# Gate logits of four steps on four column tiles of 32, turned back in one product into another PSUM bank

## The chip, the cores and the metric

The kernel runs on one core of a Trainium2 chip. The core has five engines with a queue each: PE (TensorE, products), DVE (VectorE), ACT (ScalarE), POOL (GpSimd) and SP (SyncE, which here issues DMAs). An engine takes its instructions in order and waits on semaphores. The metric is the device time of one execution in microseconds. Three runs of the kernel before took 274.95, 274.98 and 278.34 us, median 274.98.

## The reference

Two parts, one behind the other, in f32. First a recurrence over 768 tokens, for 4 sequences and 8 heads of width 48:

```
for t in range(S):
    cur = u * k_t (outer) v_t
    y[:, :, t] = r_t @ (state + cur)
    state = w * state + k_t (outer) v_t
```

Its output, as 3072 tokens of width 384, goes through a layer with 8 experts, each token to one of them:

```
do_compute = x @ w_skip > 0
logits = x[do_compute] @ w_gate            # 8 of them
e_idx = argmax(logits); gate_w = softmax(logits)[e_idx]
out = x + gate_w * (relu(x @ w1[e_idx]) @ w2[e_idx])      # where do_compute, else x
```

The eight logits and the skip score of a token are the nine numbers that this change is about.

## The kernel before, in words

*Stages.* The first stage runs over 24 steps (`NT`), numbered n: 2 pairs of sequences, 12 steps of 64 tokens each. A step handles 64 tokens of two sequences, which is 128 rows of x. The second stage computes the experts with weights that are loaded and split into a high and a low part during the first stage and behind it. Between them `route` sorts tokens to experts, from the logits in `lg`, in four groups of steps: 0 to 8, 8 to 16, 16 to 20, 20 to 24 (`GROUPS`).

*The order of work.* It is written out by hand: the loop over n issues the functions below in the order of the code, and each engine's queue holds its instructions in just that order. PE's work in step n is: `scores(n+1)` (L441, 32 records on 64x64 tiles of the array, into ps_p), `across(n+1)` (L527, state times r, into ps_y), `turn_k(n+2)` (L454, four transposes into ps_l), in some steps `gate_back`, `turn_x(n)` (L569, three transposes of x into ps_t), `state(n+1)` (L474, into ps_s), in some steps `gate_some`, and `within(n+1)` (L503, into ps_y). DVE masks the scores behind each `scores` (L462, L463), which frees ps_p and gives `within` its weights, builds rd for later steps (L411, L419) and does the many small steps of `route`. ACT copies what PE leaves in PSUM: kt (L456), xT (L572), sblk (L483), x (`evac`, L538), and makes the high parts of the weights (L113). POOL builds kd three steps ahead (L429) and the low parts (L114). SP issues the loads of dm and v five and four steps ahead, the stores of x, and one piece of expert weights a step.

*The logits.* `turn_x(n)` leaves x transposed in xT, which holds four steps (`GB`). When four are there (n = 3, 7, 11, 15, 19), `gate_some(n)` multiplies them with the gate weights wgp, zero-padded to 64 columns. Since the 384 columns of x belong to two halves c of 64 tokens, the products of c = 0 go to partitions 0 to 63 of ps_l and those of c = 1 to 64 to 127, six products in all (three parts j of the contraction), each with 256 moving columns (four steps of 64 tokens). ACT copies the result to lt. In the next step `gate_back(n)` turns it back, so that tokens lie on partitions: two products of lt with `pick`, a table of ones and zeros that also takes the nine wanted columns, into the free columns 384 and up of ps_t, the bank of `turn_x`; ACT copies from there into `lg`. A sixth call at n = 22 handles three steps (20 to 22), and its `gate_back` is issued behind the loop; the last step has a `gate` of its own (L581).

*Names.* ps_p (two banks), ps_y (two banks), ps_s, ps_r, ps_t and ps_l are all of PSUM. ps_r is used by `route` alone in the first stage (L673 to L683, L794, L796, L750), and by the experts behind it. wk, tab are pools in SBUF. A product of f32 shows in the profile as two records, an L474 of 8 products as x16.

Of the kernel before, what the change touches and what calls it, by code (L numbers as in the profile page):

```python
# [59 lines left out]
def tile_wkv_moe(  # L60
# [183 lines left out]
    with ExitStack() as actx:  # L244
# [125 lines left out]
        def setup_routes():  # L370
            nc.vector.memset(before, 0.0)
            rows = ident.rearrange("p (c q e) -> p c q e", c=2, q=NB)[:, :, :, : E + 1]
# [189 lines left out]
        gts, xcopy = {}, {}  # L562
        seen = [-1]

        def turn_x(n):
            x = xts.pop(n)
            pt = ps_t if n + 1 < NT else ps_y[:, 0]
            for c in range(NCC):
                nc.tensor.transpose(pt[:, c * P : (c + 1) * P], x[:, c * P : (c + 1) * P], ident)  # L569
            if n % GB == 0:  # L570
                gts[0] = wk.tile([P, NCC, 2, GB, C], F32, tag="xT", name=f"xT{n}", bufs=1)
            xcopy[n] = nc.scalar.copy(  # L572
                gts[0][:, :, :, n % GB, :], pt[:, :DM].rearrange("p (j c t) -> p j c t", j=NCC, c=2)
            ).ins

        def gate(n):
            half = slice(n % 2 * C, (n % 2 + 1) * C)
            pg = ps_y[half, 0, DM : DM + NB * (E + 1)]
            for j in range(NCC):
                for c in range(2):  # L580
                    nc.tensor.matmul(  # L581
                        pg,
                        gts[0][:, j, c, n % GB, :],
                        wgp[:, j, c].rearrange("p (q e) -> p q e", q=NB)[:, :, : E + 1],
                        start=(j == c == 0),
                        stop=(j == NCC - 1 and c == 1),
                    )
# [5 lines left out]
        def gate_some(n, k=GB):  # L593
            pg = ps_l[:, : k * C]
            for j in range(NCC):
                for c in range(2):
                    nc.tensor.matmul(  # L597
                        pg[c * C : (c + 1) * C, :],
                        wgp[:, j, c, :],
                        gts[0][:, j, c, :k, :].rearrange("p k t -> p (k t)"),  # L600
                        start=(j == 0),
                        stop=(j == NCC - 1),
                        skip_group_check=True,
                    )
            lt = turned_lg[n] = wk.tile([P, GB * C], F32, tag="lt", name=f"lt{n}", bufs=1)[:, : k * C]
            nc.scalar.copy(lt, pg)

        def gate_back(n, k=GB):
            lt = turned_lg.pop(n)
            w = NB * (E + 1)  # L610
            for j in range(0, k, 2):
                m = min(2, k - j) * C
                nc.tensor.matmul(
                    ps_t[:m, DM + j // 2 * w : DM + (j // 2 + 1) * w],
                    lt[:, j * C : j * C + m],
                    pick.rearrange("p q e -> p (q e)"),
                    start=True,
                    stop=True,
                )
            g0, full = n - k + 1, k // 2 * 2  # L620
            nc.scalar.copy(
                lg[:, g0 : g0 + full, :].rearrange("p n e -> p (n e)"), ps_t[:, DM : DM + full // 2 * w]
            )
            if k > full:
                nc.scalar.copy(
                    lg[:C, g0 + full : g0 + full + 2, :].rearrange("p n e -> p (n e)"),
                    ps_t[:C, DM + full // 2 * w : DM + (full // 2 + 1) * w],
# [272 lines left out]
        load_v(4)  # L900
        prep_r(2)
# [3 lines left out]
        for n in range(NT - 1):  # L905
# [368 lines left out]
def _layout(r, k, v, w, u, moe_w_skip, moe_w_gate, moe_w1, moe_w2):  # L1274
# [19 lines left out]
    gq = np.zeros((2, NB * NHP * D, NB, C // NB), wide.dtype)  # L1294
    for q in range(NB):
        gq[:, q * NHP * D : (q + 1) * NHP * D, q, : E + 1] = wide
    gq = gq.reshape(2, NCC, P, C).transpose(2, 1, 0, 3)
# [38 lines left out]
```

## Time and profile before

| | |
|---|---|
| three runs, median | 274.98 us |
| profiled execution: time, and span of its profile | 276.32 us, 274.2 us |
| PE busy | 255.6 us (93%) |
| DVE, ACT, POOL busy | 183.2, 141.1, 131.4 us |
| first stage, to the end of `within(23)` and the turning of x behind it | about 124.6 us of the span |
| granted clock of TensorE, mean | 0.998 |
| DMA over the span | 54.30 MB, mean 198 GB/s |

The profile is of one execution. A row of the chain of waits gives a start in us, a length in us, and the line whose work the end of the program depended on at that time. A row of a timeline gives start and length of a run of equal instructions, the engine, the line, the operation, the tiles (out<-in) and their shapes; in brackets stands the idle time of the engine before it and what ended that. PEld is the loading of weights into the array. Ends of PE's records are modelled, their starts are not. "128*64" ahead of a shape is the tile of the array: 128 rows, 64 columns.

### The profile page before, as it was taken

To read this page: it belongs to the slowest core of one execution; us is meant where nothing else is said; L and a number is where in the kernel's file an instruction comes from. 1 tells how busy PE (TensorE), PEld (TensorE's weight loads), DVE (VectorE), ACT (ScalarE), POOL (GpSimd) and SP (SyncE) were. 2 spreads that over 40 slices of the span, in tenths; PEclk is the share of its full clock that TensorE was granted. 3 is DMA by queue.
4 is the path that set the end of the run, shared out by engine and by line. 5 is a ranking of instruction groups with operands and counts; after the bars stand their busy time and mean duration, and the time that the engine had idled before them with its cause. 6 is when DMAs were issued, how large, how long until landed. Compare 5 with 4: busy or idle time off the path is not lost.

```text
span 274.2 us, 8740 instructions
## 1 busy us (share of the span) xinstructions
PE 255.6 (93%) x3545; PEld 233.9 (85%) x3545; DVE 183.2 (67%) x372; ACT 141.1 (51%) x316; POOL 131.4 (48%) x131
## 2 busy tenths in 40 slices
PE   7998999999979989788999999999999999999990
PEld 2797897878869877776879999999999999999990
DVE  8786657598896899954655686757748377483310
ACT  2664566667756756434455554717548085480300
POOL 8536313375545538511748853763525535255011
PEclk9999999999999999999999999999999999999999
DMA  7977678878999995435479994694837747100010
GB/s 201 308 197 240 163 203 277 248 247 256 289 274 282 272 284 159 114 93 143 111 254 308 365 379 166 219 317 145 260 121 241 241 142 261 43 4 27 15 35 23
DMA packets 31140, 54.30 MB, mean 198 GB/s; under 512 B 4535, under 2 KB 14412, under 8 KB 31088
## 3 DMA queue, kind: packets, MB, share of 16 engines
q1 hardware_dynamic: 28896, 48.19, 57.2%
q0 software_dynamic: 2048, 5.44, 5.8%
q8 instruction: 30, 0.49, 0.7%
q14 instruction: 22, 0.18, 0.2%
q10 hardware_dynamic: 144, 0.00, 0.0%
HBM read 45.82 MB, written 8.65 MB: 199 GB/s over the span
## 4 chain that ended last, share of the span: by engine, by line
PE 82%; DVE 10%; ACT 3%; issue 2%; DMA 1%; POOL 0%; POOLq 0%; ACTq 0%
PE ps_p L164 11%; PE ps_y L164 11%; PE ps_p L441 8%; PE ps_p L154 5%; PE ps_r L154 5%; PE ps_l L154 5%; PE ps_y L154 5%; PE ps_s L474 5%; PE ps_y L503 5%; PE ps_l L454 4%; PE ps_y L527 3%; PE ps_l L597 3%; PE ps_t L569 3%; PE ps_y L216 2%; PE ps_p L216 2%
## 5 line engine op out<-in xcount | busy, mean ns | idle before, releaser
L114 POOL TENSOR_TENSOR lo<-raw,hi 128x512 fp32r<-128x512 f32 x42 | 57.0, 1358 | 75.3 <-ACT hi L113 55.7
L113 ACT CAST hi<-raw 128x512 fp32r<-128x512 f32 x96 | 55.1, 624 | 0.0
L114 DVE TENSOR_TENSOR lo<-raw,hi 128x512 fp32r<-128x512 f32 x54 | 44.0, 837 | 2.6 <-ACT hi L113 2.3
L429 POOL TENSOR_TENSOR kd<-dm,w_d 128x512 f32<-128x512 f32 x22 | 30.1, 1366 | 14.7 <-DMA dm<-in_dm_dram 13.0
L172 POOL DMA_INDIRECT out_dram<-xg,sid x16 | 17.1, 1067 | 36.4 <-DVE xg L169 25.7
L462 DVE COPY_PREDICATED am<-below,ps_p 128x512 f32<-128x512 int8 x24 | 17.7, 739 | 17.1 <-PE ps_p L441 17.0
L441 PE MATMUL ps_p<-rd,kd 64*64 64x128 f32 x768 | 26.9, 276 | 0.3 <-issue 0.3
L441 PEld LDWEIGHTS ps_p<-rd,kd 64*64 64x64 f32 x768 | 20.9, 132 | 3.2 <-issue 0.7
L158 ACT ACTIVATE hh<-ps_p 128x464 fp32r<-128x464 f32 x7 | 3.9, 559 | 36.9 <-PE ps_p L154 20.1
L122 POOL DMA_INDIRECT xg<-out_dram,gid x16 | 18.2, 1139 | 8.7 <-DVE gw L694 4.0
L503 PE MATMUL ps_y<-vz,am 128*64 128x96 f32 x384 | 20.2, 247 | 2.1 <-DVE am L463 1.5
L503 PEld LDWEIGHTS ps_y<-vz,am 128*64 128x64 f32 x384 | 17.8, 137 | 3.4 <-issue 1.9
L405 ACT ACTIVATE rd<-rd,uw 128x128 f32<-128x128 f32 x52 | 17.8, 395 | 4.9 <-DVE rd L411 4.9
L474 PE MATMUL ps_s<-vz,kt 128*64 128x96 f32 x352 | 19.6, 253 | 0.0
L456 ACT COPY kt<-ps_l 128x512 f32<-128x512 f32 x22 | 12.8, 583 | 12.9 <-PE ps_l L454 12.9
L164 PE MATMUL ps_p<-hi,hh 128*128 128x384 f32 x56 | 19.4, 347 | 0.0
L164 PE MATMUL ps_y<-hi,hh 128*104 128x384 f32 x56 | 18.9, 338 | 0.0
L164 PE MATMUL ps_p<-hi,hl 128*128 128x384 f32 x56 | 18.9, 337 | 0.0
L164 PE MATMUL ps_y<-lo,hh 128*104 128x384 f32 x56 | 18.9, 337 | 0.0
L164 PE MATMUL ps_y<-hi,hl 128*104 128x384 f32 x56 | 18.9, 337 | 0.0
L164 PE MATMUL ps_p<-lo,hh 128*128 128x384 f32 x56 | 18.8, 336 | 0.0
L169 DVE SCALAR_TENSOR_TENSOR xg<-ps_y,gate_s,xg 104x384 f32<-104x384 f32 (+1 forms) x8 | 4.9, 616 | 20.5 <-PE ps_y L164 17.9
(244 smaller groups left out, 693.4 us busy)
## 6 DMA issues: line engine op xcount, KB each, us to landing
raw<-in_w_dram SPq DMA_DIRECT2D x96, 256.0 KB
dm<-in_dm_dram SPq DMA_DIRECT2D x24, 512.0 KB
vz<-in_tok_dram SPq DMA_DIRECT2D x48, 96.0 KB
out_dram<-xt SPq DMA_DIRECT2D x48, 96.0 KB
out_dram<-xt SPq DMA_DIRECT2D x4, 192.0 KB
xg<-out_dram,gid POOLq DMA_INDIRECT x16
out_dram<-xg,sid POOLq DMA_INDIRECT x16
wgp<-in_wgq_dram SPq DMA_DIRECT2D x1, 192.0 KB
```

The source lines that it names most:

```text
L113: nc.scalar.copy(hi, t)
L114: eng.tensor_tensor(lo, t, hi.bitcast(F32), ALU.subtract)
L122: ins = nc.gpsimd.indirect_dma_start(out=xg, out_offset=None, in_=out[0:rows], in_offset=bass.IndirectOffsetOnAxis(ap=gid[:, q : q + 1], a ...
L154: nc.tensor.matmul(ph, a[:, c, fs], b[:, c, :], start=(k == 0), stop=(k == 3 * NCC - 1))
L164: nc.tensor.matmul(py, a, b[:, f, :], start=(k == 0), stop=(k == 3 * NFC - 1))
L172: ins = nc.gpsimd.indirect_dma_start(out=out, out_offset=bass.IndirectOffsetOnAxis(ap=sid[:, q : q + 1], axis=0), in_=xs.pop(q), in_offset ...
L405: nc.scalar.mul(rd[:, :, 1], rd[:, :, 0], uw[:, hp : hp + 1])
L429: (eng or nc.gpsimd).tensor_tensor(kds[n], d[:, 1], w_d[:, n % NSUB, 1][:, :, None].to_broadcast([DR, NHP, 2, C]), ALU.mult,)
L441: nc.tensor.matmul(ps_p[q * C : (q + 1) * C, a, 2 * hp * C : 2 * (hp + 1) * C], kd[h, hp, q, :], rd[h, hp, q].rearrange("p s c -> p (s c)" ...
L462: nc.vector.copy_predicated(shape(am[n % 2]), below, p[:, :, 0])
L474: nc.tensor.matmul(s[a * C : (a + 1) * C, :, hp * D : (hp + 1) * D], kt[:, hp, a, :], t[:, :, a, hp, :], start=i == 0 and hp == 0, stop=Tr ...
L503: ins = nc.tensor.matmul(place_y(a, c)[:, :, g, :], am[n % 2][:, a, hp * C : (hp + 1) * C], t[:, :, a, hp, :], start=g == 0 and n % NSTEP ...
```

## The change

Five edits.

1. wgp has 32 columns for a pair of steps and half (18 are used: two sets of nine) in place of 64, so its load is 96 KB, not 192 KB. The load is issued behind `load_v(4)`, in the program's opening, where it was behind `load_v(3)`.
2. `gate_some` makes twelve products in place of six: for each j and c one for steps 0 and 1 and one for steps 2 and 3 of the four (i), each with 128 moving columns, into partitions 32(2c + i) and up of ps_l. Its result is 128 columns wide, not 256, and the copy to lt too. At n = 22 all four steps of xT are multiplied, the fourth being an old one.
3. `pick` is twice as wide, and `gate_back` makes one product of 36 columns, into the last columns of ps_r, not ps_t.
4. In the loop, `gate_some` at n = 3, 7, 11, 15 and 19 comes behind `within(n+1)` and `evac(n+1)`; at n = 22 it stays ahead of `within`.
5. xT is one fixed tile in place of one taken anew from a pool every four steps.

```diff
-        wgp = tab.tile([P, NCC, 2, C], F32, name="wgp")
-        nc.sync.dma_start(out=wgp, in_=wgq)
-        pick = tab.tile([P, NB, E + 1], F32, name="pick")
+        wgp = tab.tile([P, NCC, 2, C // 2], F32, name="wgp")
+        pick = tab.tile([P, 2, NB, E + 1], F32, name="pick")
...
         def gate_some(n, k=GB):
-            pg = ps_l[:, : k * C]
+            pg = ps_l[:, : 2 * C]
+            w = C // 2
             for j in range(NCC):
                 for c in range(2):
-                    nc.tensor.matmul(
-                        pg[c * C : (c + 1) * C, :],
-                        wgp[:, j, c, :],
-                        gts[0][:, j, c, :k, :].rearrange("p k t -> p (k t)"),
-                        start=(j == 0),
-                        stop=(j == NCC - 1),
-                        skip_group_check=True,
-                    )
-            lt = turned_lg[n] = wk.tile([P, GB * C], F32, tag="lt", name=f"lt{n}", bufs=1)[:, : k * C]
+                    for i in range(2):
+                        nc.tensor.matmul(
+                            pg[(2 * c + i) * w : (2 * c + i + 1) * w, :],
+                            wgp[:, j, c, :],
+                            xT4[:, j, c, 2 * i : 2 * i + 2, :].rearrange("p k t -> p (k t)"),
+                            start=(j == 0),
+                            stop=(j == NCC - 1),
+                            skip_group_check=True,
+                        )
+            lt = turned_lg[n] = wk.tile([P, 2 * C], F32, tag="lt", name=f"lt{n}", bufs=1)
             nc.scalar.copy(lt, pg)
 
         def gate_back(n, k=GB):
             lt = turned_lg.pop(n)
             w = NB * (E + 1)
-            for j in range(0, k, 2):
-                m = min(2, k - j) * C
-                nc.tensor.matmul(
-                    ps_t[:m, DM + j // 2 * w : DM + (j // 2 + 1) * w],
-                    lt[:, j * C : j * C + m],
-                    pick.rearrange("p q e -> p (q e)"),
-                    start=True,
-                    stop=True,
-                )
+            pb = ps_r[:, 512 - 2 * w :]
+            nc.tensor.matmul(pb, lt, pick.rearrange("p s q e -> p (s q e)"), start=True, stop=True)
...
         load_v(4)
+        nc.sync.dma_start(out=wgp, in_=wgq)
         prep_r(2)
...
-            if n < TE and n % GB == GB - 1:
-                gate_some(n)
-            elif n == NT - 2:
+            if n == NT - 2:
                 gate_some(n, NT - 1 - TE)
             within(n + 1, kcopy.get(n + 2, xcopy[n]))
             evac(n + 1)
+            if n < TE and n % GB == GB - 1:
+                gate_some(n)
             if back:
                 back()
```

How this stands on PE, from `turn_x(3)` in step 3 to `state(5)` in step 4, in the kernel before; kd, rd, kt, xt and the like carry numbers of their buffers:

```order
L569 MATMUL ps_t<-ident,xt_523 128x128 x3
L474 MATMUL ps_s<-vz_128,kt_495 64x2x48 x8
L597 MATMUL ps_l<-xT_333,wgp 64x256 x6
L503 MATMUL ps_y<-vz_128,am_151 64x2x48 x8
L441 MATMUL ps_p<-rd_503,kd_501 64x128 x16
L527 MATMUL ps_y<-sblk_200,rd_503 64x48 x16
L454 MATMUL ps_l<-ident,kd_582 128x128 x4
L613 MATMUL ps_t<-pick,lt_602 128x18 x2
L569 MATMUL ps_t<-ident,xt_612 128x128 x3
L474 MATMUL ps_s<-vz_129,kt_576 64x2x48 x8
```

The same stretch of PE in the changed kernel, whose lines are numbered a little lower (L453 is `turn_k`, L473 `state`, L502 `within`, L440 `scores`, L526 `across`):

```order
L569 MATMUL ps_t<-ident,xt_523 128x128 x3
L473 MATMUL ps_s<-vz_128,kt_495 64x2x48 x8
L502 MATMUL ps_y<-vz_128,am_150 64x2x48 x8
L597 MATMUL ps_l<-xT_200,wgp 32x128 x12
L440 MATMUL ps_p<-rd_503,kd_501 64x128 x16
L526 MATMUL ps_y<-sblk_199,rd_503 64x48 x16
L453 MATMUL ps_l<-ident,kd_582 128x128 x4
L612 MATMUL ps_r<-pick,lt_620 128x36
L569 MATMUL ps_t<-ident,xt_604 128x128 x3
L473 MATMUL ps_s<-vz_129,kt_576 64x2x48 x8
```

L597 has moved from between L474 and L503 to between L503 and L441, with twelve products of half the columns on half the width; `gate_back`'s product has become one, into ps_r.

On ACT, from the copy of xT in step 3 to the copy of lg in step 4, before:

```order
L572 COPY xT_333<-ps_t 128x6x64
L483 COPY sblk_200<-ps_s 128x384
L606 COPY lt_602<-ps_l 128x256
L538 COPY xt_612<-ps_y 128x384
L405 ACTIVATE rd_584<-rd_584,uw 128x2x64 x2
L456 COPY kt_662<-ps_l 128x512
L621 COPY lg<-ps_t 128x36
```

And in the changed kernel:

```order
L570 COPY xT_200<-ps_t 128x6x64
L482 COPY sblk_199<-ps_s 128x384
L537 COPY xt_604<-ps_y 128x384
L606 COPY lt_620<-ps_l 128x128
L404 ACTIVATE rd_584<-rd_584,uw 128x2x64 x2
L455 COPY kt_668<-ps_l 128x512
L614 COPY lg<-ps_r 128x36
```

The copy of lt now stands behind the copy of x, ahead of the bonus (L404), and lg is read from ps_r; kt's copy is still ahead of lg's.

More of the change, by code (lines that the diff above doesn't have):

```diff
@@ L371, in setup_routes @@
             nc.vector.memset(before, 0.0)
-            rows = ident.rearrange("p (c q e) -> p c q e", c=2, q=NB)[:, :, :, : E + 1]
+            rows = ident.rearrange("p (c s q e) -> p c s q e", c=2, s=2, q=NB)[:, :, :, :, : E + 1]
             nc.vector.tensor_tensor(pick, rows[:, 0], rows[:, 1], ALU.add)
@@ L560, in put_x @@
                 x_out.append(ins.ins)
-        gts, xcopy = {}, {}
+        xT4 = tab.tile([P, NCC, 2, GB, C], F32, name="xT4")
+        xcopy = {}
         seen = [-1]
@@ L569, in turn_x @@
                 nc.tensor.transpose(pt[:, c * P : (c + 1) * P], x[:, c * P : (c + 1) * P], ident)
-            if n % GB == 0:
-                gts[0] = wk.tile([P, NCC, 2, GB, C], F32, tag="xT", name=f"xT{n}", bufs=1)
             xcopy[n] = nc.scalar.copy(
-                gts[0][:, :, :, n % GB, :], pt[:, :DM].rearrange("p (j c t) -> p j c t", j=NCC, c=2)
+                xT4[:, :, :, n % GB, :], pt[:, :DM].rearrange("p (j c t) -> p j c t", j=NCC, c=2)
             ).ins
@@ L582, in gate @@
                         pg,
-                        gts[0][:, j, c, n % GB, :],
+                        xT4[:, j, c, n % GB, :],
                         wgp[:, j, c].rearrange("p (q e) -> p q e", q=NB)[:, :, : E + 1],
@@ L610, in gate_back @@
             w = NB * (E + 1)
-            for j in range(0, k, 2):
-                m = min(2, k - j) * C
-                nc.tensor.matmul(
-                    ps_t[:m, DM + j // 2 * w : DM + (j // 2 + 1) * w],
-                    lt[:, j * C : j * C + m],
-                    pick.rearrange("p q e -> p (q e)"),
-                    start=True,
-                    stop=True,
-                )
+            pb = ps_r[:, 512 - 2 * w :]
+            nc.tensor.matmul(pb, lt, pick.rearrange("p s q e -> p (s q e)"), start=True, stop=True)
             g0, full = n - k + 1, k // 2 * 2
-            nc.scalar.copy(
-                lg[:, g0 : g0 + full, :].rearrange("p n e -> p (n e)"), ps_t[:, DM : DM + full // 2 * w]
-            )
+            nc.scalar.copy(lg[:, g0 : g0 + full, :].rearrange("p n e -> p (n e)"), pb[:, : full // 2 * w])
             if k > full:
                 nc.scalar.copy(
-                    lg[:C, g0 + full : g0 + full + 2, :].rearrange("p n e -> p (n e)"),
-                    ps_t[:C, DM + full // 2 * w : DM + (full // 2 + 1) * w],
+                    lg[:C, g0 + full : g0 + full + 2, :].rearrange("p n e -> p (n e)"), pb[:C, full // 2 * w :]
                 )
@@ L1293, in _layout @@
     wide = np.concatenate([moe_w_gate, moe_w_skip[:, None]], axis=1).reshape(2, NHP * D, E + 1)
-    gq = np.zeros((2, NB * NHP * D, NB, C // NB), wide.dtype)
+    gq = np.zeros((2, NB * NHP * D, NB, C // 2 // NB), wide.dtype)
     for q in range(NB):
         gq[:, q * NHP * D : (q + 1) * NHP * D, q, : E + 1] = wide
-    gq = gq.reshape(2, NCC, P, C).transpose(2, 1, 0, 3)
+    gq = gq.reshape(2, NCC, P, C // 2).transpose(2, 1, 0, 3)
     return {
```

## Prediction

> **What bounds the kernel now.** I began with the page (span and busy shares), then took the busy times of three stretches, the last ending with the span.
>
> ```profile
> span 274.2 us, 8740 instructions
> PE 255.6 (93%) x3545; PEld 233.9 (85%) x3545; DVE 183.2 (67%) x372; ACT 141.1 (51%) x316; POOL 131.4 (48%) x131
> ```
>
> ```profile
> 0.00:124.60 124.60, 113.66 (x2532) 97.16 (x2532) 97.74 (x216) 73.01 (x175) 61.88 (x74) 1.00 0.77 226
> 135.00:274.20 139.20, 132.49 (x953) 129.39 (x952) 79.53 (x129) 64.13 (x129) 64.73 (x53) 1.00 0.54 179
> ```
>
> The columns are busy time of PE, its weight loads, DVE, ACT and POOL, the granted clock, DMA share and GB/s. The change lies wholly in the first 125 us. PE is busy 91% there and 95% in the expert stage behind, where DMA stands at 0.54: what the first stage gives back, the second should hand on.
>
> Next, the chain of waits from the first gate step on: one step that holds a `gate_some` (n = 3), one that holds a `gate_back` (n = 4), and the beginning of a plain one (n = 5).
>
> ```profile
> 27.24 0.33 PE ps_t L569 x3
> 27.57 1.03 PE ps_s L474 x16
> 28.60 1.29 PE ps_l L597 x12
> 29.89 0.66 PE ps_y L503 x16
> 30.55 1.03 PE ps_p L441 x32
> 31.59 0.45 PE ps_y L527 x32
> 32.04 0.60 PE ps_l L454 x4
> 32.66 0.59 ACT kt L456
> 33.39 0.55 PE ps_t L569 x3
> 33.94 0.81 PE ps_s L474 x16
> 34.75 0.66 PE ps_y L503 x16
> 35.41 1.03 PE ps_p L441 x32
> 36.44 0.45 PE ps_y L527 x32
> 36.89 0.59 PE ps_l L454 x4
> 37.48 0.33 PE ps_t L569 x3
> 37.81 0.81 PE ps_s L474 x16
> ```
>
> Nearly every piece is PE, one behind the other. A plain step is 0.59 + 0.33 + 0.81 + 0.66 + 1.03 + 0.45 = 3.87 us. `gate_some` (L597) stands in the chain with its whole length. `gate_back` makes L454 to L474 take 33.94 - 32.04 = 1.90 us, where the plain step takes 37.81 - 36.89 = 0.92. It costs 0.98: its own four records, and then a wait, named in the list of waits.
>
> ```profile
> PE ps_t L569 <- ACT lg L621: 2.1, 5, 0.5
> ```
>
> Five times the turning of x waits for the copy of the logits, which ACT runs only behind the copy of kt; both use ps_t.
>
> **The change part by part.** *How long 24 records on four column tiles take.* An f32 product shows as two records. L569 runs three records of 128 columns in the whole array in 0.33: 0.109 each, one at a time. L441 has 32 records of 128 columns on tiles of 64x64. L454, the first of its shape behind L527, takes 0.59 where 4 x 0.109 = 0.44 would do, so a change of tile shape costs 0.15; L474 against L503, the same records without a change ahead, gives 0.81 - 0.66 = 0.15 again. Less that, L441 is 0.88, or 8 x 0.11: four run at a time. L597 before has 12 records of 256 columns in 1.29, 0.215 for each pair: two tiles, two at a time. So the array runs as many records at once as it has tiles in every shape that the trace shows; for 128x32 no row exists. By the nearest, L441, 24 records are 6 x 0.109 = 0.65, and because the shape now changes between L503 and L597 as well as behind it, 0.15 more: 0.80. The other ends are two at a time, 12 x 0.109 + 0.15 = 1.46, and one at a time, 24 x 0.109 + 0.15 = 2.77. I take 0.80.
>
> The Trainium skill (TensorE: Matmul & The Clock Gate, Part 3, measured speedup) speaks against the full four: three column tiles of 32 were measured at 2.38 times, not 3. By that ratio, as an estimate, `gate_some` would be 0.97 and the sum below some 0.7 smaller. The trace's four 64x64 tiles show no such loss, and no run here yet shows 128x32.
>
> *What `gate_some` costs before, call by call.* At n = 3, L474 is lengthened too: 1.03 + 1.29 - 0.81 = 1.51. The other calls:
>
> ```profile
> 47.04 1.43 PE ps_l L597 x12
> ...
> 64.44 1.29 PE ps_l L597 x12
> ...
> 84.80 1.29 PE ps_l L597 x12
> ...
> 104.31 1.44 PE ps_l L597 x12
> ...
> 121.59 1.20 PE ps_l L597 x12
> ```
>
> Against 0.80 this saves 0.71, 0.63, 0.49, 0.49 and 0.64. The call at n = 22 has 192 columns, and keeps its place: six pairs, each 64 columns and so 0.05 shorter, less 0.15 for the shape: 0.15.
>
> *What `gate_back` costs behind the change.* One product, two records. Its price is its weight load:
>
> ```profile
> 32.35 0.53 PEld L613 LDWEIGHTS ps_t<-pick,lt 128*128 128x128 f32 x4
> L613 PEld LDWEIGHTS ps_t<-pick,lt x24: 133/192/192, 32.4 to 124.7; 128*128 128x128 f32 x22, 128*64 128x64 f32 x2
> ```
>
> Four loads of 0.19 begin within 0.53, so one each 0.113: two are 0.22. As the target is ps_r, L569 follows at once; kt's copy and lg's run beside L569 and L474. Saved: 0.98 - 0.22 = 0.76 on PE per call; at n = 23 two loads fewer, 0.2.
>
> *The moved places.* `gate_some` behind `within` and `evac` makes ACT copy lt behind xt.
>
> ```profile
> 29.93 0.37 ACT L606 COPY lt<-ps_l 128x256 f32<-128x256 f32 x1 [0.76 <-PE ps_l L597]
> ```
>
> The next L454 writes ps_l and must wait for that copy. The copy can start 0.80 behind L503 and a few tenths of draining, and ends by 1.5; L454 comes 0.80 + 1.03 + 0.45 = 2.28 behind L503, so 0.8 is free. Behind lt on ACT stand the split of a weight piece, the bonus and kt, none needed before L454's end. The load of wgp, half as large, lets dm(4), x(0)'s stores and v(4) pass on SP's queue, and stands ahead of dm(5), whose use is POOL's kd:
>
> ```profile
> 20.70 1.28 POOL L429 TENSOR_TENSOR kd<-dm,w_d 128x512 f32<-128x512 f32 x1 [2.81 <-DMA dm<-in_dm_dram]
> ```
>
> It ends at 21.98; PE turns it just ahead of 27.24, five us later. I put the move at nothing: without that cover it would cost the time of 96 KB, some tenths. wgp itself is first read behind 28.6.
>
> *Where PE stops being the bound.* The DVE rows of mask_scores tell how long DVE stood idle waiting for the scores; that is what PE can gain there before DVE is last.
>
> ```profile
> 36.51 0.74 DVE L462 COPY_PREDICATED am<-below,ps_p 128x512 f32<-128x512 int8 x1 [2.32 <-PE ps_p L441]
> ...
> 55.09 0.74 DVE L462 COPY_PREDICATED am<-below,ps_p 128x512 f32<-128x512 int8 x1 [0.89 <-PE ps_p L441]
> ...
> 67.49 0.75 DVE L462 COPY_PREDICATED am<-below,ps_p 128x512 f32<-128x512 int8 x1 [0.61 <-PE ps_p L441]
> ...
> 72.40 0.74 DVE L462 COPY_PREDICATED am<-below,ps_p 128x512 f32<-128x512 int8 x1 [0.64 <-PE ps_p L441]
> ...
> 92.71 0.74 DVE L462 COPY_PREDICATED am<-below,ps_p 128x512 f32<-128x512 int8 x1 [0.50 <-PE ps_p L441]
> ...
> 96.58 0.74 DVE L462 COPY_PREDICATED am<-below,ps_p 128x512 f32<-128x512 int8 x1 [0.17 <-PE ps_p L441]
> ...
> 109.09 0.73 DVE L462 COPY_PREDICATED am<-below,ps_p 128x512 f32<-128x512 int8 x1
> ...
> 110.75 0.21 DVE L801 TENSOR_TENSOR lists<-ps_r,lists 128x48 f32<-128x48 f32 x1 [0.16 <-PE ps_r L796]
> ```
>
> The 0.76 of n = 4 fits whole into the idle time of the mask behind it (2.32), that of n = 8 too (0.89). The 0.49 of `gate_some` at n = 11 fits (0.61). Of the 0.76 at n = 12 only 0.64 does; at n = 16 0.50, and 0.17 more in the next step, 0.67. From 96.6 to 110.6 DVE itself is the bound, routing the second group: at 109.09 it comes from its own work, without idle time. So of the 0.64 + 0.76 at n = 19 and 20 only the 0.16 of the last row arrives. That also hides the one wait that the new bank adds: at n = 20 L794 and L796 write ps_r behind lg's copy.
>
> Sum: (0.71 + 0.76) + (0.63 + 0.76) + (0.49 + 0.64) + (0.49 + 0.67) + 0.16 + (0.15 + 0.2) = 5.66 us. The profiled execution took 276.32 (span 274.2 and 2.1 around it), so 270.7 for one like it; the median of the three runs is 274.98, 0.5% lower, so 269.3. I write 269.4.
>
> **The rivals.**
>
> *Two tiles at a time* (0.10). `gate_some` is 1.46: next to nothing gained by it at n = 3 and 7, 0.17 lost at 11 and 15, 0.5 lost at 22. `gate_back` still gives 0.76, 0.76, 0.64, 0.67, 0.16 and 0.2. Together 2.4: 272.6. Against it stands L441.
>
> *One tile at a time: slower* (0.03). `gate_some` is 2.77, a loss of 1.26, 1.34, 1.48 and 1.48 against 0.76 won in each following step; n = 19 loses some 0.4 behind DVE, n = 22 1.8 - 0.2. Together 4.5 lost: 279.5. It decides from 80 ns per record on, since (1.29 + 0.76 - 0.15) / 24 = 0.08, that is where fewer than 1.4 tiles overlap. No shape in the trace does that.
>
> *DVE takes over earlier* (0.17). Its small steps of routing are stretched when POOL works beside them; L801 above takes 0.21 for 128x48, this one, also small, 1.23:
>
> ```profile
> 94.12 1.23 DVE L670 TENSOR_TENSOR oh<-eq,m 128x64 bf16<-128x64 f32 x1
> ```
>
> Let two such stretches more fall between 55 and 96 us, and the gains of the third and fourth group (1.13 + 1.16) are gone: 271.7.
>
> *A stall of PE's own goes* (0.10). The chain holds, before any gate, idle time of PE for which the profile shows no cause:
>
> ```profile
> 21.29 1.04 issue
> ```
>
> With other DMA traffic at that time (wgp gone from ahead of dm(4)) it may vanish: 268.4. It may as well come again elsewhere, with 48 weight loads and records in a call where 24 were; that is inside the range.
>
> *The forecast's case* has 0.60.
>
> **How the numbers follow.** 269.4 is the likeliest. Its own spread is about one us each way (stretched DVE steps, a stall more or less), 268.2 to 270.6. The range, 267.6 to 272.8, adds the case without the stall below and the two cases of smaller gain above; it leaves out the slow case and the tails. About 2% is what a measurement of this kernel can tell from no change: below 269.48 or above 280.48. Half of the forecast's case and the one without the stall lie below: 0.43 faster; slower by 2% needs one tile at a time and more, 0.02; 0.55 within.
>
> **What would show it.** L597 with 24 records in about 0.65 to 0.8 of the chain, starts of four close together; 1.3 or 2.6 would be the rivals. L569 behind `gate_back` without the wait for lg, and L454 to L474 in about 1.14 at n = 4. The mask rows with less idle time: next to none at n = 13 and 17, and at n = 20 DVE still without any. PE's stall at 21.3 there or not. The end of the first stage some 5.7 us earlier, and the expert stage as long as before. Wrong would be: L454 waiting for lt's copy, PE waiting on ps_r, or a first stage that gains and an expert stage that gives it back.

## The result, and the profile after

Over 20 runs of each the changed kernel's median is 276.4 us (273.35 to 278.47), that of the kernel before 276.71 us (274.95 to 278.34). The ratio is 0.9938, 95% interval 0.991 to 0.9967: some 1.7 us faster (0.0062 x 276.7), which is no change by the bound of 2%. Forecast were 269.4 us and a gain of 5.66. Some executions of every kernel ran disturbed; the medians hold them, the ratios leave them out and say more, and no distance between masks is taken below from the profile of such an execution. The profiled execution took 274.48 us against 276.32.

The page of the profile, and busy times of the same two stretches as in the prediction, with the bounds moved by the 3.04 us by which the first stage ends earlier (columns as there):

```profile
span 272.6 us, 8873 instructions
PE 254.6 (93%) x3604; PEld 234.0 (86%) x3605; DVE 185.0 (68%) x372; ACT 139.8 (51%) x316; POOL 129.8 (48%) x131
```

```profile
0.00:121.56 121.56, 111.27 (x2594) 95.98 (x2595) 99.66 (x216) 71.72 (x175) 61.31 (x74) 0.97 0.78 231
131.96:272.58 140.62, 133.84 (x960) 130.60 (x958) 79.30 (x129) 64.29 (x129) 63.49 (x53) 0.99 0.54 176
```

The first stage is 3.04 us shorter, the expert stage 1.42 longer (140.62 against 139.20). The granted clock is no longer 1.00 in either (0.97 and 0.99).

The chain of waits over the three steps that the prediction showed (a step with `gate_some`, one with `gate_back`, the beginning of a plain one):

```profile
26.07 0.81 PE ps_s L473 x16
26.88 0.66 PE ps_y L502 x16
27.54 0.79 PE ps_l L597 x24
28.33 1.03 PE ps_p L440 x32
29.36 0.45 PE ps_y L526 x32
29.81 0.59 PE ps_l L453 x4
30.40 0.15 PE ps_r L612 x2
30.55 0.36 PE ps_t L569 x3
30.91 0.81 PE ps_s L473 x16
```

`gate_some` takes 0.79 (forecast 0.80), and L453 to L473 is 30.91 - 29.81 = 1.10 (forecast 1.14, before 1.90). Up to here the change does what was expected.

How far each kernel has come is read from the start of DVE's first mask row. I number masks by the step whose scores they mask; mask n+1 is issued in step n.

| mask | before | after | ahead | what lies between |
|---|---|---|---|---|
| 3 | 21.05 | 20.90 | 0.15 | |
| 4 | 26.27 | 24.77 | 1.50 | PE's stall of its own at 21.29 is gone |
| 5 | 31.65 | 29.43 | 2.22 | `gate_some`, n = 3: 0.72 |
| 6 | 36.51 | 33.48 | 3.03 | `gate_back`, n = 4: 0.81 |
| 8 | 44.91 | 41.22 | 3.69 | another stall of before, at 44, is gone |
| 10 | 55.09 | 49.93 | 5.16 | n = 7 and 8: 0.66 + 0.81 |
| 12 | 62.56 | 58.34 | 4.22 | a new stall of PE, 0.9 |
| 14 | 72.40 | 66.83 | 5.57 | n = 11 and 12: 0.49 + 0.86 |
| 17 | 87.85 | 81.77 | 6.08 | n = 15: 0.51 |
| 18 | 92.71 | 86.58 | 6.13 | `gate_back`, n = 16: 0.05 |
| 20 | 101.87 | 96.34 | 5.53 | 0.60 lost |
| 21 | 109.09 | 104.74 | 4.35 | 1.18 lost |
| 22 | 115.73 | 112.88 | 2.85 | 1.50 lost |

By mask 17 the changes proper have given 0.72 + 0.81 + 0.66 + 0.81 + 0.49 + 0.86 + 0.51 = 4.86. Stalls of PE, which no term held, add 1.35 + 0.66 - 0.94 = 1.07. Then 3.28 us are lost between masks 18 and 22 (23.02 become 26.30), and 1.4 behind the turning of xg, the first transposes of gathered tokens (L145, 120.34 against 123.38 us).

*Mask 20 to 21.* DVE's timeline of after:

```profile
100.92 0.29 DVE L779 TENSOR_TENSOR vl<-oj,id 128x128 fp32r<-128x128 f32 x1
101.13 1.36 DVE L779 TENSOR_TENSOR vl<-oj,gh 128x128 fp32r<-128x128 f32 x1
102.42 1.35 DVE L779 TENSOR_TENSOR vl<-oj,gl 128x128 fp32r<-128x128 f32 x1
103.69 0.68 DVE L410 TENSOR_TENSOR rd<-dm,w_d 128x512 f32<-128x512 f32 x1
```

and POOL's:

```profile
101.03 1.32 POOL L114 TENSOR_TENSOR lo<-raw,hi 128x512 fp32r<-128x512 f32 x1 [0.29 <-ACT hi L113]
102.31 1.31 POOL L428 TENSOR_TENSOR kd<-dm,w_d 128x512 f32<-128x512 f32 x1
```

Of three equal steps of routing the one that begins before POOL's operation takes 0.29 us; the other two begin behind the start of one and end just behind its end. In the kernel before the same three (L789 there) ran while POOL was idle, from 106.27 to 107.54:

```profile
106.46 0.29 DVE L789 TENSOR_TENSOR vl<-oj,id 128x128 fp32r<-128x128 f32 x1
106.67 0.28 DVE L789 TENSOR_TENSOR vl<-oj,gh 128x128 fp32r<-128x128 f32 x1
106.87 0.28 DVE L789 TENSOR_TENSOR vl<-oj,gl 128x128 fp32r<-128x128 f32 x1
...
107.79 1.38 DVE L419 TENSOR_TENSOR rd<-rd,uw 128x256 f32<-128x256 f32 x1
```

```profile
104.00 2.27 POOL L429 TENSOR_TENSOR kd<-dm,w_d 128x512 f32<-128x512 f32 x1
107.54 1.35 POOL L114 TENSOR_TENSOR lo<-raw,hi 128x512 fp32r<-128x512 f32 x1 [1.26 <-PE ps_p L441]
```

POOL's part was late enough to miss them, and stretched one L419 instead (1.38 us, where after's L418 at 104.40 takes 0.43). With PE ahead, ACT's high part and POOL's low part come sooner beside DVE, and two steps are stretched by 1.08 and 1.07; less the 0.95 of the L419 that is 1.20, and 1.18 were lost. The Trainium skill (SBUF — State Buffer, Who interferes with whom) states the mechanism: a DVE instruction with two SBUF inputs and a GpSimd one that reads SBUF share a port pair, and the later one blocks until the earlier ends. The rows agree: each stretched step ends about 0.15 us behind POOL's operation (101.13 + 1.36 against 101.03 + 1.32, 102.42 + 1.35 against 102.31 + 1.31).

*Mask 21 to 22.* PE's timeline and ACT's of after:

```profile
102.15 0.53 PE L569 MATMUL ps_t<-ident,xt 128*128 128x128 f32 x3
105.70 0.17 PE L784 MATMUL ps_r<-before,ones 128*128 128x8 bf16 x1 [3.03 <-ACT lg L614]
105.73 1.88 PE L786 MATMUL ps_r<-vl,ol 128*128 128x48 f32 x8
```

```profile
104.40 0.69 ACT L404 ACTIVATE rd<-rd,uw 128x128 f32<-128x128 f32 x2 [3.45 <-DVE rd L410]
105.00 0.56 ACT L455 COPY kt<-ps_l 128x512 f32<-128x512 f32 x1
105.47 0.19 ACT L614 COPY lg<-ps_r 128x36 f32<-128x36 f32 x1
```

PE stands still for 3.03 us. The lists of the second group (L784, L786) write ps_r and so wait for the copy of lg, which stands on ACT behind kt's copy and the bonus; the bonus waits for DVE's rd, behind the stretched steps. This is the wait that the prediction called hidden. What follows is seen in the busy times by stretch (the granted clock is the third number from the end):

```profile
98.60:102.05 3.45, 3.45 (x112) 3.08 (x109) 3.45 (x5) 1.75 (x5) 3.16 (x2) 1.00 0.86 268
102.05:105.46 3.41, 0.63 (x7) 0.46 (x6) 3.38 (x5) 1.06 (x3) 1.57 (x2) 1.00 0.62 173
105.46:112.29 6.83, 6.58 (x78) 6.29 (x81) 5.02 (x22) 2.77 (x9) 1.92 (x2) 0.50 0.31 86
112.29:129.40 17.11, 15.64 (x241) 12.31 (x236) 10.16 (x42) 6.84 (x18) 4.83 (x5) 1.00 0.43 112
129.40:132.80 3.40, 3.40 (x12) 3.11 (x11) 1.04 (x5) 0.66 (x2) 2.67 (x3) 0.50 0.64 182
```

A stretch of 3.41 us in which PE was busy for 0.63 is followed by 6.83 us at half clock; 17.11 us behind these come 3.40 more. The first half clock costs DVE another wait (L791, 1.49 us, for L786), the second falls into the expert stage.

### The profile page after: what moved, and what is told of

It reads as the page before. It is cut to its first block, busy times and chain, and to the rows that moved or that the text cites. A ratio compares the mean times of both kernels' runs of the same rounds, so it can differ in the third digit from the quotient of the medians.

```text
span 272.6 us, 8873 instructions
## 1 busy us (share of the span) xinstructions
PE 254.6 (93%) x3604; PEld 234.0 (86%) x3605; DVE 185.0 (68%) x372; ACT 139.8 (51%) x316; POOL 129.8 (48%) x131
## 4 chain that ended last, share of the span: by engine, by line
PE 76%; DVE 16%; ACT 3%; issue 2%; DMA 1%; POOL 0%; POOLq 0%
PE ps_p L164 11%; PE ps_y L164 11%; PE ps_p L440 6%; PE ps_p L154 5%; PE ps_r L154 5%; PE ps_l L154 5%; PE ps_y L154 5%; PE ps_y L502 5%; PE ps_s L473 4%; PE ps_l L453 3%; PE ps_y L526 2%; DVE rd L410 2%; PE ps_p L216 2%; DVE am L461 2%; PE ps_t L569 2%
## 5 line engine op out<-in xcount | busy, mean ns | idle before, releaser
L114 POOL TENSOR_TENSOR lo<-raw,hi 128x512 fp32r<-128x512 f32 x42 | 56.0, 1332 | 73.6 <-ACT hi L113 71.3
L440 PE MATMUL ps_p<-rd,kd 64*64 64x128 f32 x768 | 27.3, 281 | 0.0
L440 PEld LDWEIGHTS ps_p<-rd,kd 64*64 64x64 f32 x768 | 21.4, 136 | 3.1 <-issue 1.2
L502 PE MATMUL ps_y<-vz,am 128*64 128x96 f32 x384 | 20.9, 252 | 1.9 <-DVE am L462 1.5
L404 ACT ACTIVATE rd<-rd,uw 128x128 f32<-128x128 f32 x52 | 17.7, 395 | 7.6 <-DVE rd L410 7.6
L502 PEld LDWEIGHTS ps_y<-vz,am 128*64 128x64 f32 x384 | 17.9, 141 | 2.8 <-issue 1.9
L473 PE MATMUL ps_s<-vz,kt 128*64 128x96 f32 x352 | 20.0, 258 | 0.0
L410 DVE TENSOR_TENSOR rd<-dm,w_d 128x512 f32<-128x512 f32 x24 | 19.6, 816 | 0.0
```

Source lines behind the costliest of these rows:

```text
L114: eng.tensor_tensor(lo, t, hi.bitcast(F32), ALU.subtract)
L404: nc.scalar.mul(rd[:, :, 1], rd[:, :, 0], uw[:, hp : hp + 1])
L410: nc.vector.tensor_tensor(rds[n][:, :, :, 0], d[:, 0], w_d[:, n % NSUB, 0][:, :, None].to_broadcast([DR, NHP, 2, C]), ALU.mult,)
L440: nc.tensor.matmul(ps_p[q * C : (q + 1) * C, a, 2 * hp * C : 2 * (hp + 1) * C], kd[h, hp, q, :], rd[h, hp, q].rearrange("p s c -> p (s c)" ...
L473: nc.tensor.matmul(s[a * C : (a + 1) * C, :, hp * D : (hp + 1) * D], kt[:, hp, a, :], t[:, :, a, hp, :], start=i == 0 and hp == 0, stop=Tr ...
L502: ins = nc.tensor.matmul(place_y(a, c)[:, :, g, :], am[n % 2][:, a, hp * C : (hp + 1) * C], t[:, :, a, hp, :], start=g == 0 and n % NSTEP ...
```

## The experiments

Two theories stood at first. W: the wait in step 20 and the half clock behind it lose the gain. D: between masks 18 and 22 DVE sets the pace and gives the gain back, through POOL's operations beside its steps. For each kernel I give the median of its runs, the ratio to the kernel before on the same chip with its interval, and, where it can be compared, the distance from mask 18 to mask 22 in the one profile that there is of each (before 23.02, after 26.30).

**The bank alone, and the tiles alone.** The kernel before with `gate_back`'s two products in ps_r:

```diff
-                    ps_t[:m, DM + j // 2 * w : DM + (j // 2 + 1) * w],
+                    ps_r[:m, 476 + j // 2 * w : 476 + (j // 2 + 1) * w],
```

> The kernel before, with one part of the change: gate_back's two products go to the last columns of ps_r, not of ps_t; gate_some, its place, wgp and pick are as before. By the terms of the prediction PE saves the wait of L569 for lg but keeps the four records: 0.98 - 0.43 = 0.55 us in each of the steps 4, 8, 12 and 16, little at 20, so about 2.2 us, a ratio to before of 0.992. Theory W (in the changed kernel the gain was lost at step 20, where PE waits for lg's copy before it may write ps_r, sits idle for 3 us, and then has half its clock): here PE arrives at step 20 only some 2 to 3 us early, idle time there under 2 us, full clock, so the 2.2 us arrive. Theory D (from step 17 to 22 DVE sets the pace and gives back what PE brings, whatever PE does): at the end 1 us or less, 0.996 or more.

The changed kernel with its one product in the old bank:

```diff
-            pb = ps_r[:, 512 - 2 * w :]
+            pb = ps_t[:, DM : DM + 2 * w]
```

> The changed kernel, with gate_back's one product in the old bank ps_t (columns 384 to 419). L569 should wait for lg's copy again, 0.4 to 0.6 us in each of the steps 4, 8, 12, 16, and at step 20 the wait should stand before L569 in place of L784. PE then comes to step 20 some 2.4 us less early than in the changed kernel. Theory W: the idle time at step 20 is about 3 us less 2.4, no half clock, and the time is the same as or better than that of the changed kernel, ratio to before 0.990 to 0.994, although PE has more waits. Theory D: what is left of PE's gain at step 17 (about 4 us) is cut to the same 1.5 us: 0.994.

Measured: the bank alone 273.08 us, 0.9888 (0.9829 to 0.9947); the tiles alone 275.95 us, 0.986 (0.9773 to 0.9946). In the latter L569 waits for lg 0.6 to 0.7 us in steps 4, 8, 12 and 16, and 3.39 in step 20. By the ratios neither half is worth less than both together (0.9938; the intervals overlap, and the second ratio rests on two runs): their gains don't add. And the wait in step 20 is no matter of the bank: in the old one L569 takes it in place of L784.

**The wait and the idle time of step 20.** First the changed kernel with 14 idle products, some 3 us, ahead of the turning of x in step 20, so that the wait stays and the idle time goes:

```diff
+            if n == TE:
+                warm(14)
             turn_x(n)
```

> The changed kernel, with 14 bf16 products of ones (512 columns, into ps_t, never read) on PE in step 20, ahead of the transposes of turn_x(20), where PE would be idle for 3 us: they take 14 x 0.216 = 3.0 us. The wait stays, the idle time goes. Theory W: the granted clock stays at 1.0 there; L786 takes 0.8 us and not 1.5, DVE's wait before L791 falls from 1.49 to about 0.7 us, and the products behind it (L473, L502, L440) take 0.7 to 0.9 us and not 1.3 to 1.8; the first stage ends 1.5 to 2 us earlier than in the changed kernel, ratio to before 0.987. Theory D: DVE is the pace there, half clock or not: at most 0.7 us, 0.991.

Then the changed kernel with the bonus of step 22 issued behind that turning, so that lg's copy no longer stands behind it:

```diff
-            if 0 < n and n + 2 < NT:
+            late = n == TE
+            if 0 < n and n + 2 < NT and not late:
                 bonus(n + 2, BH)
...
             turn_x(n)
+            if late:
+                bonus(n + 2, BH)
```

> The changed kernel, with ACT's bonus(22) (L404, which waits for DVE's rd) issued behind turn_x(20), in step 20 alone, so that the copies of kt, lg and xT no longer stand behind it on ACT. Theory W: lg's copy comes right behind kt's, at about 103 us and not 105.5, L784 and L786 then wait only for DVE's last vl, idle time on PE about 1.2 us, full clock; L791 follows DVE's masks without idle time, 1.5 us earlier than in the changed kernel: ratio to before 0.987. Theory D: the stretched DVE steps at 101 to 104 us stay; the gain is what DVE stood idle there, 1.5 us, and no more; if another wait takes its place (scores(22) for the later bonus), less than 0.5: 0.992.

Measured: 273.9 us, 0.9927 (0.9893 to 0.9961), and 273.67 us, 0.9894 (0.9838 to 0.9951). The fill leaves no half clock behind step 20:

```profile
100.00:114.00 14.00, 12.88 (x259) 10.25 (x258) 13.07 (x32) 6.99 (x19) 8.17 (x6) 1.00 0.56 158
```

With the bonus moved, L784 waits 0.26 us for lg in place of 3.03, and one window of half clock is left in place of two, which its expectation did not have:

```profile
104.77 0.17 PE L784 MATMUL ps_r<-before,ones 128*128 128x8 bf16 x1 [0.26 <-ACT lg L614]
105.65 1.07 PE L786 MATMUL ps_r<-vl,ol 128*128 128x48 f32 x8 [0.72 <-DVE vl L779]
```

```profile
108.31:111.72 3.41, 3.18 (x53) 2.97 (x55) 3.20 (x17) 1.71 (x5) 2.17 (x2) 0.50 0.43 130
```

Both bring masks 18 to 22 from 26.30 to 24.24 and 24.29. From mask 21 to 22 8.14 becomes 6.69 and 6.06; from mask 20 to 21 it is 8.40 in all three; the other 0.61 of the fill's gain lie between masks 18 and 20, ahead of its edit. So in the profiles W is worth 1.5 to 2.1 us of the 3.28; in the times the intervals of 0.9927 and 0.9894 overlap with that of 0.9938. Some 1.2 to 1.8 us are left for D.

How firm such a distance is can be told from four profiles of kernels that are equal up to mask 21: the changed kernel, the two of this pair, and a mended one that follows below. From mask 20 to 21 they take 8.40, 8.40, 8.40 and 8.41 us, where the kernel before and its version with the bank and three idle products (also below) take 7.22 and 7.21. From mask 18 to 20 the four take 9.76, 9.15, 9.83 and 11.07, the two 9.16 and 9.18. So the 1.18 us between masks 20 and 21 come again each time, while in a changed kernel the whole distance can move by up to 2 us without any edit.

**POOL beside DVE.** The kernel with the bonus moved, with the split of the weight piece in step 20 also moved behind the turning of x, so that POOL comes later:

```diff
             if late:
                 bonus(n + 2, BH)
+                piece(n - FIRST_LOAD - LEAD, split=True)
```

> The changed kernel, in which at step 20 the bonus of step 22 and then the split of a weight piece (ACT's high part, POOL's low part) are issued behind the turning of x. Theory S: POOL's low part beside DVE's small steps at L779 stretches these from 0.28 to 1.36 us each, so from the mask of step 20 to that of 21 8.40 us fall to 6.0 to 7.4, and from the mask of 18 to that of 22 24.3 (with the bonus moved alone) become 22.5 to 23.4. Rival P: it is the other work of POOL or of the DMA queues at that time; then 8.40 stays, or POOL's next operation stretches the same steps, and 24.3 stays within 0.5.

Measured: 276.35 us, 0.9955 (0.9913 to 0.9997). Mask 20 to 21 is 6.24, as S had it, but masks 18 to 22 are 25.24, more than either theory had: 10.51 from 18 to 20, ahead of the edit, and 14.73 from 20 to 22, where the bonus moved alone gave 14.46. DVE's and POOL's rows of this kernel tell why:

```profile
103.30 0.29 DVE L779 TENSOR_TENSOR vl<-oj,gh 128x128 fp32r<-128x128 f32 x1
...
106.80 1.12 DVE L808 SCALAR_TENSOR_TENSOR sid<-lists,em 128x8 uint32<-128x8 f32 x1
...
108.03 1.15 DVE L640 SCALAR_TENSOR_TENSOR rdo<-lg,rev 128x32 f32<-128x32 f32 x1
109.11 0.18 DVE L649 TENSOR_TENSOR eq<-lg,mx 128x32 f32<-128x32 f32 x1
```

```profile
106.60 1.30 POOL L114 TENSOR_TENSOR lo<-raw,hi 128x512 fp32r<-128x512 f32 x1 [3.70 <-ACT hi L113]
107.86 1.27 POOL L428 TENSOR_TENSOR kd<-dm,w_d 128x512 f32<-128x512 f32 x1
```

The vl steps are short again, and POOL's two operations have met two others, of 128x8 and 128x32. The place of the stretch moves; its amount stays (21 to 22 takes 8.49 in place of 6.06), since DVE has such steps queued one behind the other.

The slower time has another cause beside it. PE was busy for 1.45 us of the window ahead of 111.50, and then had three windows at half clock:

```profile
108.09:111.50 3.41, 1.45 (x61) 1.43 (x64) 3.31 (x9) 1.52 (x5) 3.19 (x3) 1.00 0.45 115
111.50:121.74 10.24, 9.63 (x133) 8.45 (x124) 6.16 (x21) 1.97 (x5) 1.66 (x2) 0.50 0.40 110
```

From mask 22 to 23 that makes 6.84 us, where the kernel with the bonus moved takes 4.43.

Next, on top of that, the whole bonus on ACT in steps 16 to 20, issued behind the turning of x in all five, which takes five DVE operations out of that stretch:

```diff
+            late = 16 <= n <= TE
...
+            if late:
+                bonus(n + 2, 0)
...
-            if n + 3 < NT:
+            if n + 3 < NT and not 18 <= n + 3 <= 22:
                 prep_r(n + 3, (1,))
```

> As the run before, and in steps 16 to 20 the whole of the bonus on ACT, so that DVE's part of it (L418, 0.4 us or up to 1.4 us each) goes in five steps. Theory D (DVE sets the pace from the mask of 17 to that of 22 and gives back what PE gained): these two masks come closer by 1.5 to 2.5 us and the time falls by 1 to 2 us more. Rival C: PE or the wait for kt sets the pace there by now; then the distance stays within 0.4, and what ACT has more (0.4 us a step) shows as a later kt.

Measured: 278.13 us, 0.9991 (0.9943 to 1.0039), masks 25.79 apart. D in this form is wrong: with less work on DVE the stretch did not shrink (from mask 17 to 22 30.40 for 29.43), and DVE now idles twice between masks 18 and 19:

```profile
90.37 0.69 DVE L410 TENSOR_TENSOR rd<-dm,w_d 128x512 f32<-128x512 f32 x1 [0.66 <-DMA dm<-in_dm_dram]
91.99 0.73 DVE L461 COPY_PREDICATED am<-below,ps_p 128x512 f32<-128x512 int8 x1 [0.92 <-PE ps_p L440]
```

The first of these waits is for a load of dm. It comes, with 0.7 to 0.9 us, in four profiles of changed kernels (this one, the one without low parts, the mended one and the early split) and in none of the kernel before compared here: a lead of PE can also run into the loads, which no run here separates. As I read it, PE, ACT and DVE are so close there that none of them alone is the bound.

Then POOL's low parts of steps 17 to 20 left out (zeros in their place, written where DVE idles), in the changed kernel with the bonus moved and in the kernel before:

```diff
+            if split and 17 <= n <= 20:
+                nc.scalar.copy(his[e % 2][:, j * QC : (j + 1) * QC], raw.pop((e, j)))
+            elif split:
                 split_piece(e, j, nc.gpsimd)
```

> The changed kernel with the bonus of step 22 behind the turning of x in step 20, and in steps 17 to 20 no low part of the weight piece: POOL's subtraction is left out and those four low parts are zeros, written by DVE in steps 6 to 9, where it idles. Work is left out, so the time counts only beside the next run. Theory D (from mask 18 to mask 22 DVE sets the pace, and POOL's operations stretch its small steps by 1.0 to 1.1 us each): 24.29 us between these masks become 21 to 22, and the turning of xg comes 2 to 3 us earlier than without the edit. Rival K: the stretches come from POOL's kd and from the port whoever uses it, or PE sets the pace; then 24.29 changes by less than 0.6.

> The kernel before with the same four low parts left out. By D the distance between the masks of 18 and 22 falls from 23.02 to about 21 here too, DVE being the bound in both, and the changed kernel without them then lies 3 us or more below this one (269 to 270.5 against 273 to 274.5). By K it stays near 23.0, and both kernels lie as far apart as with the low parts.

Measured: 271.69 us, 0.9801 (0.974 to 0.9862), masks 22.78 apart; and 275.62 us, 0.9962 (0.9937 to 0.9986), masks 22.42 apart. The three vl steps take 0.28 to 0.29 in the changed kernel. Its distance falls by 1.5 (expected 2.3 to 3.3), that of the kernel before by 0.6 only (expected 2), and the turning of xg comes 1.2 us earlier (expected 2 to 3): smaller than D had it, larger than K. But what the changed kernel loses on the one before between these masks is now 22.78 - 22.42 = 0.36 us, in place of 3.28, or 1.27 with the bonus moved. And from mask 20 to 21 they now take the same, 5.62 and 5.60, where it was 8.40 and 7.22. In the times the two lie 1.6% or 4.4 us apart (0.0161 x 276, with 0.7% either way by the two intervals), where with the low parts it was 0.6%, or 1.05% with the bonus moved. So without POOL's low parts the difference between masks 20 and 21 is gone. That they cost the changed kernel more than the one before in the whole time is likely and not shown: against the kernel with the bonus moved, the gain is within the noise.

Last, all work kept, but the splits begun two steps earlier and none in steps 19 and 20, again in both kernels:

```diff
+        counts = [n >= 5 and n not in (19, 20) for n in range(NT - 1)]
...
-            if n >= FIRST_LOAD + LEAD:
-                piece(n - FIRST_LOAD - LEAD, split=True)
+            for j in SPLITS[n]:
+                piece(j, split=True)
```

> The changed kernel with the bonus of step 22 behind the turning of x, and the split of weight pieces (load, high part, POOL's low part) begun two steps earlier, in step 5 in place of 7, with none in steps 19 and 20. All work is done. If it is the place of POOL's operations beside DVE's steps of routing that costs, 24.3 us from mask 18 to mask 22 become 21.5 to 23, and the ratio to before falls to 0.980 to 0.986. If it is the amount of POOL's work or of DMA, what is saved there comes back in steps 5 and 6 or in 21 to 23, and the ratio stays near 0.989.

> The kernel before with the same early split of weight pieces, none in steps 19 and 20. If DVE between masks 18 and 22 sets the pace in both kernels, about 1 us between these masks goes here too (23.0 becomes 21.5 to 22.3), and this kernel lies 2.5 to 4 us behind the changed one of this call (ratio to before 0.993 to 0.998). If not, both lie as far apart as with the old places, 1 us or less.

Measured: 273.89 us, 0.9893 (0.9851 to 0.9934), masks 23.69 apart (expected 21.5 to 23); and 279.05 us, 1.0011 (0.9971 to 1.0051; expected 0.993 to 0.998). The two kernels lie 1.2% apart (3.3 us), inside the 2.5 to 4 that D expected. But the changed kernel gains nothing over the one with the bonus moved alone (0.9894): its ratio is where the rival had it, although its profile, of its fastest run, shows a span of 269.8 us. And the kernel before gets no faster. So this pair does not show what POOL's place costs in the whole time, nor that the change is worth more where POOL is out of the way: 1.2% with 0.6% either way does not differ from the 1.05% of the bonus moved alone.

**The half clock at the end of the first stage.** The kernel with bonus and piece moved, with three idle products ahead of the gathering of the last tokens; then the same with the bonus on ACT:

```diff
+        warm(3)
         next(last)
         gather(E, wpool)
```

> As the first run of this call, with three idle products on PE ahead of the gathering of tokens for the last group, where PE waits about 0.5 us for the last route. Theory H: the short waits around 123 to 129 us bring the half clock of 3.41 us at 129 to 133, which lengthens L194 from 0.785 to 1.175 and L216 from 1.04 to 1.92; with the filling there is no half clock there, and the end of the program stands as far ahead as the turning of xg does (2.1 us becomes 3.2 or more), 1.2 us less in all. Rival N: the half clock has to do with the longer wait near 121 to 123 us or with nothing that 0.3 us of products can change; then it stays, with the time of the first run of this call.

> Both of the last two edits together. By D and H: 3 us below the changed kernel with the bonus moved alone, some 270.5 to 271.5 as the median, ratio 0.978 to 0.985 against before. By C and N: as the first run of this call.

Measured: 275.21 us, 0.9928 (0.9892 to 0.9963), and 275.9 us, 0.9906 (0.9866 to 0.9946). The runs could not tell H from N: neither profile has a half clock at 129 to 133 us, but the kernel without the fill has none either. (Up to the fill the first of the two is the kernel with bonus and piece moved, and it repeats the half clock behind mask 21, from 111.78 to 118.61.) What a half clock there costs is read across the profiles: from the turning of xg to the last product of PE after loses 1.36 us on before and the kernel with the bonus moved 1.30, both with it; those with piece and bonus moved, with and without the fill, gain 0.27 to 0.28. That is 1.6 us. The 3 us expected of the last kernel did not come.

**Mended versions.** The changed kernel with the bonus moved, four idle products ahead of the turning of x in step 20 and three ahead of the last gathering; the kernel before with the bank alone and those three; and the early split with all seven idle products:

> The changed kernel with the bonus of step 22 behind the turning of x, four idle products on PE ahead of that turning and three ahead of the gathering of the last tokens. If what is lost behind the first stage is the half clock alone, none shows at 108 to 112 nor at 129 to 133 us, the last product of PE stands as far ahead of before's as the turning of xg does (within 0.4 us), and the median is 1.2 to 1.8 us below that of the kernel with the bonus moved alone: ratio 0.982 to 0.987. If the half clock has another cause, it comes again, and the ratio stays at 0.989 or above.

> The kernel before with its two products of gate_back sent to the end of ps_r and three idle products ahead of the gathering of the last tokens: the bank's part of the change without the four column tiles. If the four tiles bring to the end what they save in the first stage, this run lies 2 us behind the one before it; if DVE takes their saving back between the masks of 18 and 22, both lie within 0.7 us of each other, at a ratio of 0.985 to 0.99.

> The first kernel of this call with the idle products of the mended one (four ahead of the turning of x in step 20, three ahead of the gathering of the last tokens). If a half clock behind step 20 or behind the last route is left in the first kernel of this call, it goes and the time falls by 1 to 1.5 us (ratio 0.976 to 0.981); if none is left there, the ratio is that of the first kernel within 0.003.

Measured: 274.09 us, 0.9889 (0.9851 to 0.9926); 274.97 us, 0.9906 (0.9866 to 0.9946); 273.21 us, 0.9895 (0.9852 to 0.9938). The profile of the first has no half clock before the program's end, and its last product stands 2.63 us ahead of before's, where the turning of xg is 2.35 ahead: the expected picture, but not the expected 0.982 to 0.987, and masks 18 to 22 are 25.39 apart, 11.07 of them ahead of its edits. The bank alone is 0.2% behind the whole change, 0.5 us with 1.5 either way (0.9 us by the medians), between what the two theories had: of what the four tiles save in the first stage (0.72 + 0.66 + 0.49 + 0.51 = 2.4) not all reaches the end, and perhaps little. At mask 20 this kernel is 2.10 us ahead of before, and its L794 in step 20 does not wait for lg at all: the long wait of the changed kernel comes with its larger lead (5.53), not with the bank by itself. The third is as fast as the early split without idle products (0.9893), whose profile has no half clock before the end either. Some 1.1% is what the change is worth with its own wait mended, no more than the first measurement of the bank alone (0.9888); no kernel here that does all the work got clearly beyond that.

## Why the prediction was wrong, step by step

- *24 records on four column tiles*: right, 0.79 for 0.80. The weight loads have a median of 110 ns and come four at a time; the rivals of two and one tile at a time are out, and so is 0.97, worked out from the Trainium skill's 2.38 for three tiles (TensorE: Matmul & The Clock Gate, Part 3).
- *`gate_back`*: right. 0.81 and 0.81 measured for 0.76 at n = 4 and 8, and the wait of L569 for lg is gone.
- *The terms up to mask 17*: 4.48 forecast (0.71 + 0.76 + 0.63 + 0.76 + 0.49 + 0.64 + 0.49), 4.86 measured. The caps by DVE's idle time did not hold: at n = 12 0.86 came where the cap was 0.64, and at n = 16 0.05 came of 0.67. There a step of routing (L640, before's L650) took 1.32 us in place of 0.78. The 1.07 us that the stalls of PE gave on top are luck of the two profiled executions.
- *The moved places*: right in that L453 waits for no copy of lt; the chain has it directly behind L526.
- *"From 96.6 to 110.6 DVE itself is the bound"*: this step failed. The reading was right, the use of it wrong: the stretch was taken to be as long as before, with only the gains inside it lost. It grew by 3.28 us. 1.50 of these, between masks 21 and 22, go with the wait of the next item and the half clock behind it; with either mended that part fell by 1.45 or 2.08. 1.18 come between masks 20 and 21, where, beside the oj step (1.36 and 1.38 us), two of DVE's steps meet POOL's operations and in the kernel before one did: the length of the stretch depends on which steps meet them, and with PE ahead POOL's low part comes earlier beside DVE's. What moved the other 0.60, between masks 18 and 20, differs from profile to profile and stays open. The rival "DVE takes over earlier" named the stretching by POOL and priced it as two stretches, but as a loss of two gains between 55 and 96 us; 2.68 of the 3.28 came behind mask 20 (96.34), in the stretch that the forecast had set aside.
- *"That also hides the one wait that the new bank adds"*: this step failed too, and "PE waiting on ps_r" was one of the prediction's own signs of being wrong. At n = 20 PE is so far ahead of DVE that the wait is 3.03 us. The order of ACT's queue was on the table (lg's copy behind kt's, kt's behind the bonus), and what the bonus waits for was not followed: DVE's rd, in just the stretch where DVE is late.
- *"The expert stage as long as before"*: wrong by 1.4 us, the half clock at 129.4 to 132.8. It is the other sign that the prediction named, a first stage that gains and an expert stage that gives back; what brings this half clock stays open.
- *A stall of PE's own*: it did go (1.35 us between masks 3 and 4), one at 44 us went too (0.66), and one of 0.9 came at 54 us, row below. The chance of 0.10 was for its going alone. In other profiles of the changed kernels such stalls stand elsewhere, so that its going has to do with the moved load is not shown.
- *The base*: 274.98 was a median of three. Over 20 runs the kernel before has 276.71, so 1.7 us of the 7.0 by which the time was missed (276.4 for 269.4) are the base and not the change.

## What to carry to other kernels

Where several engines are nearly even in a stretch, time saved ahead of it does not simply arrive or vanish: it shifts their queues against each other, and the stretch itself can grow (here from 23.02 to 26.30 us). One profile of each kernel is little to judge such a stretch by: compare profiles of equal code first. Before a wait is called hidden, follow the releaser's queue to the engine that is last there, and ask whether a lead on one side makes the wait longer. Two engines that share a port are to be read as one timeline: moving an operation away from one victim only pays if no other stands next in the queue.

## What the runs showed of the hardware

- *The clock.* The two half clocks of after begin at 105.46 and 129.40, seven times 3.42 us apart, and last two such windows and one. The Trainium skill states the window (TensorE: Matmul & The Clock Gate, Part 1: 3413 ns, running freely), and the trace agrees. It also has half the clock come after an idle window, which the trace bears out for 102.05, nearly idle with PE busy for 0.63 us, and not for 126.00. Four windows of after on that grid:

```profile
71.30:74.70 3.40, 1.89 (x32) 1.57 (x32) 3.33 (x8) 1.54 (x4) 2.59 (x2) 1.00 0.64 155
74.70:78.10 3.40, 3.40 (x91) 3.23 (x86) 2.93 (x6) 2.73 (x7) 1.14 (x1) 1.00 0.99 332
126.00:129.40 3.40, 2.60 (x16) 2.09 (x17) 2.51 (x14) 1.10 (x2) 1.66 (x2) 1.00 0.07 24
129.40:132.80 3.40, 3.40 (x12) 3.11 (x11) 1.04 (x5) 0.66 (x2) 2.67 (x3) 0.50 0.64 182
```

  1.89 us of busy PE are followed by the full clock, 2.60 by half. With the bonus moved 2.10 and 2.49 (104.90 and 125.37) are followed by half, too. What is counted stays open.

- *Stalls of PE without a cause in the program.* Most profiles have some, of 0.2 to 1.5 us, in the middle of a group of records. After's longest, in the list of PE's waits:

```profile
PE ps_l L453 <- issue: 0.9, 1, 0.9
```

  They fall at places that lie a multiple of 256 records of PE and PEld apart (before's at the 706th, those with the bonus moved at the 962nd and 1218th, and so on), at other multiples from run to run. The transfers of instructions on one queue come in packets of some 16 KB (31 for 0.51 MB in after); whether the stalls are the waiting for a next packet was not tested, nor how much they add to the spread of equal runs (273.35 to 278.47 us for after).

- *Four tiles at once.* 24 f32 records of 128 columns on 128x32 tiles take as long as six would one behind the other, and a change of shape more: 6 x 0.109 + 0.15 = 0.80, measured 0.79.
